# Scaled B and C variants of a state-space layer by TensorE rotation matrices, parameters by row loads

## Chip, cores, metric

The kernel runs on one core of one Trainium2 chip. The metric is device time in microseconds (us); lower is better. Executions of one kernel on one chip agree within two per cent here (the kernel before took 228.98 to 233.16 us in its widest group of runs), and each experiment below is compared with executions of the kernel before on the same chip. Engines are called by their names: TensorE (PE in the profile; PEld is its weight load), VectorE (DVE), ScalarE (ACT), GpSimd (POOL), SyncE (SP). ACTq and SPq are those engines' DMA issues.

## The reference

Two independent layers share the input length of 2048; their outputs stand side by side. Part A is a complex diagonal state-space layer, part B a sliding, dilated attention.

```python
# part A: 448 states, 448 features
dt = jnp.exp(log_dt)
Lam_bar = jnp.exp(dt * Lam)
B_bar = ((Lam_bar - 1.0) / Lam)[:, None] * Bmat
Bu = jnp.einsum("bld,pd->blp", x + 0j, B_bar)
for t in range(L):                      # h = Lam_bar * h + Bu[t], kept for every t
    ...
y = 2.0 * jnp.einsum("blp,dp->bld", hseq, Cmat).real + x * Dskip[None, None, :]
# part B: 16 heads of 28; each position sees 8 positions, 2 apart
logits = jnp.einsum("bhsd,bhswd->bhsw", q, kg) * scale
attn = _softmax(jnp.where(mask, logits, -1e9), axis=-1)
o = jnp.einsum("bhsw,bhswd->bhsd", attn, vg)   # then @ wo
```

The kernel takes part A in blocks. It needs four scaled variants of B (B times the powers 0, -1, -2, -3 of `Lam_bar`, with the factor of the third line) and three of C (times the powers 1, 2, 3). A state's real and imaginary parts are in partitions p and p + 64 of one of seven blocks `m`, so multiplying by a complex number mixes two partitions: it is a 2x2 rotation (with a scaling) for each state.

In what follows projection g makes q, k and v for group g of positions, units g are the four head groups of that group, and `wo` is the output projection. Part A runs in the order B variants, first layer, scan (the matrices `Mm` are its constants), `hfull`, `y`. An eviction is a copy out of PSUM, where the matmuls of these kernels leave their results.

## The kernel before

```python
# attention unit: one of 4 head groups of one of 5 groups of positions (cut)
def unit(self, gi, hg):
    ...                                   # scores by TensorE into s_ps
    for u in range(2):
        nc.scalar.activation(pt[...], sp[u][...], ACT.Exp, scale=scale)
        G.affine_select(out=pv, in_=pv, ...)      # band mask, one side
        G.affine_select(out=pv, in_=pv, ...)      # band mask, other side
    ...                                   # o_ps by TensorE
    V.transpose(tO, po); V.reciprocal(r, ...)
    V.tensor_tensor(on, tO, r, op=ALU.mult)       # both inputs in SBUF
    V.transpose(oT[:, hg, 0:tot], on)

# B variants: Re and Im swapped copy bY, then a multiply-add on VectorE, then a DMA transpose
def loads_b(self):
    ...
    for sl, v in ((slice(0, PL), bre_v), (slice(PL, P), bim_v)):
        nc.scalar.dma_start(self.bX[sl, :, 0:384], v[:, :, 0:384])
        nc.scalar.dma_start(self.bX[sl, :, 448:512], v[:, :, 384:448])
    nc.sync.dma_start(self.bY[0:PL], self.bX[PL:P])
    nc.sync.dma_start(self.bY[PL:P], self.bX[0:PL])

def b_variant(self, s):
    for m in range(NM):                                   # NM = 7
        # st = bX * sa   (ScalarE for even m, VectorE for odd m)
        eng.scalar_tensor_tensor(st[:, m, :], self.bY[:, m, :], self.sb[:, s, m:m + 1], st[:, m, :],
                                 op0=ALU.mult, op1=ALU.add)
    nc.sync.dma_start_transpose(self.Bv[s][:], st[:].rearrange("p m c -> p (m c)"))

# parameters: a column of two-byte elements for each partition
def loads_params(self):
    for src, name in ((self.A_Lre, "lre"), (self.A_Lim, "lim"), (self.A_logdt, "ldt")):
        v = src.rearrange("(m p) -> p m", p=PL)
        nc.sync.dma_start(raw[0:PL], v)
        nc.sync.dma_start(raw[PL:P], v)
    ...                                                   # dsk_raw in the same way

# ten matrices of powers for the scan: 128x896 each, two SBUF inputs, on GpSimd
def mats(self, eng):
    for i in range(NMAT):
        eng.tensor_tensor(self.M[:, i], self.Dm[...broadcast...], self.Sc[:, i]...broadcast..., op=ALU.mult)

# order of the program
b.loads(); a.loads_params(); b.load_x(0, 1); a.loads_b(); b.load_x(1, 0); b.load_x(1, 1)
b.prep(); a.setup(); b.proj(0); a.b_variant(0); a.loads_c()
for hg in range(4): b.unit(0, hg)
b.proj(1); a.b_variant(1); a.loads_x(); a.b_variant(2); b.loads2(); a.b_variant(3); a.mats(G)
for hg in range(4): b.unit(1, hg)
...     # projection 2, units 2 with the first layer l1, projection 3, scan l2, units 3,
...     # c_variants, hfull, y with units 4, output projections wo
```

The softmax here doesn't subtract the row's maximum and nothing guards it: scores larger than these inputs give would overflow.

Of the kernel before, what the change touches and what calls it, by code (L numbers as in the profile page):

```python
# [34 lines left out]
NMAT = len(MATS)  # L35

# [9 lines left out]
class PartB:  # L46
# [8 lines left out]
    def loads(self):  # L55
        nc, pool, G = self.nc, self.pool, self.nc.gpsimd
        self.xb = [pool.tile([P, KT, XC], bf16, name=f"xb{p}", tag=f"xb{p}") for p in range(2)]
        self.load_x(0, 0)
        self.wqk = pool.tile([P, KT, 2 * D], bf16, name="wqk_nat", tag="r3")
        self.wv = pool.tile([P, KT, D], bf16, name="wv")  # L60
        G.memset(self.wqk[0:64, 3, :], 0.0)
        G.memset(self.wv[0:64, 3, :], 0.0)
        w = self.B_wqkv
        nc.scalar.dma_start(self.wqk[:, 0:3, :], w[0:384, 0:2 * D].rearrange("(k p) c -> p k c", p=P))
        nc.scalar.dma_start(self.wqk[64:128, 3, :], w[384:448, 0:2 * D])
        nc.scalar.dma_start(self.wv[:, 0:3, :], w[0:384, 2 * D:].rearrange("(k p) c -> p k c", p=P))
        nc.scalar.dma_start(self.wv[64:128, 3, :], w[384:448, 2 * D:])
# [17 lines left out]
    def prep(self):  # L85
        nc, pool, V, G = self.nc, self.pool, self.nc.vector, self.nc.gpsimd
        for p in range(2):
            G.memset(self.xb[p][:, :, 0:XP], 0.0)
            G.memset(self.xb[p][:, :, XP + 1024:], 0.0)
        self.wp = pool.tile([P, 2, KT, H, 32], bf16, name="wqk_p", tag="wqk_p")  # L90
        G.memset(self.wp[:, :, :, :, DH:], 0.0)
# [4 lines left out]
    def proj(self, gi):  # L96
        nc, pool = self.nc, self.pool
# [17 lines left out]
        for w, segs, dst in ((0, qs, qT), (1, ks, kT)):  # L115
            for hg in range(4):
# [9 lines left out]
                n += 1  # L126
        nc.gpsimd.memset(va[:, :, :, DH:], 1.0)
        for i, (p, i0, _) in enumerate(blocks):
# [5 lines left out]
            if i % 2 == 0:  # L134
                nc.scalar.copy(va[:, i, :, 0:DH], ps[:])
            else:
                nc.vector.tensor_copy(va[:, i, :, 0:DH], ps[:])
# [58 lines left out]
class PartA:  # L196
# [8 lines left out]
    def loads_params(self):  # L205
        nc, pool = self.nc, self.pool
        self.raw = []
        for src, name in ((self.A_Lre, "lre"), (self.A_Lim, "lim"), (self.A_logdt, "ldt")):
            raw = pool.tile([P, NM], bf16, name=name + "_raw")
            v = src.rearrange("(m p) -> p m", p=PL)  # L210
            with nc.allow_non_contiguous_dma(reason="tiny param vector"):
                nc.sync.dma_start(raw[0:PL], v)
                nc.sync.dma_start(raw[PL:P], v)
            self.raw.append(raw)
        self.dsk_raw = pool.tile([P, KT], bf16, name="dsk_raw")
        with nc.allow_non_contiguous_dma(reason="tiny param vector"):
            nc.sync.dma_start(self.dsk_raw[:, 0:3], self.A_Dskip[0:384].rearrange("(k p) -> p k", p=P))
            nc.sync.dma_start(self.dsk_raw[:, 3:4], self.A_Dskip[320:448].rearrange("(k p) -> p k", p=P))

    def loads_b(self):  # L220
        nc, pool = self.nc, self.pool
        self.bX = pool.tile([P, NM, 512], bf16, name="bX", tag="r0")
        self.bY = pool.tile([P, NM, 512], bf16, name="bY", tag="r1")
        nc.gpsimd.memset(self.bX[:, :, 384:448], 0.0)
        bre_v = self.A_Bre.rearrange("(m p) d -> p m d", p=PL)
        bim_v = self.A_Bim.rearrange("(m p) d -> p m d", p=PL)
        for sl, v in ((slice(0, PL), bre_v), (slice(PL, P), bim_v)):
            nc.scalar.dma_start(self.bX[sl, :, 0:384], v[:, :, 0:384])
            nc.scalar.dma_start(self.bX[sl, :, 448:512], v[:, :, 384:448])
        nc.sync.dma_start(self.bY[0:PL], self.bX[PL:P])  # L230
        nc.sync.dma_start(self.bY[PL:P], self.bX[0:PL])
# [9 lines left out]
    def loads_c(self):  # L241
        nc, pool = self.nc, self.pool
        cn = pool.tile([112, 4, NM, 2, PL], bf16, name="cn", tag="c7")
        with nc.allow_non_contiguous_dma(reason="interleaving re and im columns"):
            for ri, src in enumerate((self.A_Cre, self.A_Cim)):
                for a in range(4):
                    nc.gpsimd.dma_start(cn[:, a, :, ri, :],
                                        src[112 * a:112 * (a + 1)].rearrange("p (m q) -> p m q", q=PL))
        self.cP = pool.tile([P, NM, D], bf16, name="cP")
        self.cQ = pool.tile([P, NM, D], bf16, name="cQ")  # L250
        for a in range(4):
            nc.sync.dma_start_transpose(self.cP[:, :, 112 * a:112 * (a + 1)],
                                        cn[:, a].rearrange("p m r q -> p (m r q)"))
        nc.sync.dma_start(self.cQ[0:PL], self.cP[PL:P])
        nc.sync.dma_start(self.cQ[PL:P], self.cP[0:PL])

    def setup(self):
# [6 lines left out]
        lre, lim, ldt = sm("lre"), sm("lim"), sm("ldt")  # L264
        for t_, r_ in zip((lre, lim, ldt), self.raw):
            V.tensor_copy(t_[:], r_[:])
        dsk = sm("dsk", (P, KT))
        V.tensor_copy(dsk[:], self.dsk_raw[:])
        dt_bf = pool.tile([P, NM], bf16, name="dt_bf")
        nc.scalar.activation(dt_bf[:], ldt[:], ACT.Exp)  # L270
# [6 lines left out]
        V.tensor_tensor(arg[:], dt[:], lre[:], op=ALU.mult)  # L277
        th = sm("th")
        V.tensor_tensor(th[:], dt[:], lim[:], op=ALU.mult)
# [33 lines left out]

        lm1, den, t0, t1, rden = sm("lm1"), sm("den"), sm("t0"), sm("t1"), sm("rden")
        V.tensor_scalar(lm1[:], la_re, -1.0, None, op0=ALU.add)
        V.tensor_tensor(den[:], lre[:], lre[:], op=ALU.mult)
        V.tensor_tensor(t0[:], lim[:], lim[:], op=ALU.mult)
        V.tensor_tensor(den[:], den[:], t0[:], op=ALU.add)
        V.reciprocal(rden[:], den[:])
        sa, sb, tb = sm("sa", (P, 4, NM)), sm("sb", (P, 4, NM)), sm("tb", (P, 3, NM))  # L320
        g_re, g_im = sa[:, 0, :], sb[:, 0, :]
        V.tensor_tensor(g_re, lm1[:], lre[:], op=ALU.mult)
        V.tensor_tensor(t1[:], la_im, lim[:], op=ALU.mult)
        V.tensor_tensor(g_re, g_re, t1[:], op=ALU.add)
        V.tensor_tensor(g_re, g_re, rden[:], op=ALU.mult)
        V.tensor_tensor(g_im, la_im, lre[:], op=ALU.mult)
        V.tensor_tensor(t1[:], lm1[:], lim[:], op=ALU.mult)
# [3 lines left out]
        b3 = [P, 3, NM]  # L331
# [7 lines left out]
        V.tensor_scalar(sb[0:PL], sb[0:PL], -1.0, None, op0=ALU.mult)  # L339
        self.sa, self.sb = sa, sb  # L340
        self.ca, self.cb = sm("ca", b3), sm("cb", b3)
        V.tensor_scalar(self.ca[0:PL], pw_re[0:PL, 0:3, :], 2.0, None, op0=ALU.mult)
        V.tensor_scalar(self.ca[PL:P], pw_re[PL:P, 0:3, :], -2.0, None, op0=ALU.mult)
        V.tensor_scalar(self.cb[:], pw_im[:, 0:3, :], -2.0, None, op0=ALU.mult)
# [6 lines left out]
        Sc = pool.tile([P, NMAT, NM, 2], bf16, name="Sc")  # L351
        V.tensor_copy(Sc[0:PL, :, :, 0], pw_re[0:PL, 3:13])
        V.tensor_scalar(Sc[PL:P, :, :, 0], pw_im[PL:P, 3:13], -1.0, None, op0=ALU.mult)
        V.tensor_copy(Sc[0:PL, :, :, 1], pw_im[0:PL, 3:13])
        V.tensor_copy(Sc[PL:P, :, :, 1], pw_re[PL:P, 3:13])  # L355
        self.Sc = Sc
        self.Dg = pool.tile([P, KT, P], bf16, name="Dg")
        for k in range(KT):
            V.tensor_scalar(self.Dg[:, k, :], ident[:], dsk[:, k:k + 1], None, op0=ALU.mult)
        V.memset(self.Dg[0:PL, 3, :], 0.0)  # L360

    def mats(self, eng):
        self.M = self.pool.tile([P, NMAT, NM, 2, PL], bf16, name="Mm")
        for i in range(NMAT):
            eng.tensor_tensor(self.M[:, i], self.Dm[:].unsqueeze(1).unsqueeze(1).to_broadcast([P, NM, 2, PL]),  # L365
                              self.Sc[:, i].unsqueeze(3).to_broadcast([P, NM, 2, PL]), op=ALU.mult)
# [4 lines left out]
    def b_variant(self, s):  # L371
        nc, pool, eng = self.nc, self.pool, self.nc.vector
        if s == 0:
            self.Bv = [None] * 4
        st = pool.tile([P, NM, 512], bf16, name="st", tag=("r2" if s % 2 == 0 else "r3"))
        for m in range(NM):
            if m % 2 == 0:
                nc.scalar.activation(st[:, m, :], self.bX[:, m, :], ACT.Copy, scale=self.sa[:, s, m:m + 1])  # L378
            else:
                eng.tensor_scalar(st[:, m, :], self.bX[:, m, :], self.sa[:, s, m:m + 1], None, op0=ALU.mult)  # L380
            eng.scalar_tensor_tensor(st[:, m, :], self.bY[:, m, :], self.sb[:, s, m:m + 1], st[:, m, :],  # L381
                                     op0=ALU.mult, op1=ALU.add)
        self.Bv[s] = pool.tile([P, NM * KT, P], bf16, name=f"Bv{s}", tag=f"Bv{s}")
        nc.sync.dma_start_transpose(self.Bv[s][:], st[:].rearrange("p m c -> p (m c)"))

    def c_variants(self):
        nc, pool = self.nc, self.pool
        self.Dv = [self.cP]
        for s in range(1, 4):
            d = pool.tile([P, NM, D], bf16, name=f"Dv{s}", tag=f"Bv{s}")  # L390
            for m in range(NM):
                nc.scalar.activation(d[:, m, :], self.cP[:, m, :], ACT.Copy, scale=self.ca[:, s - 1, m:m + 1])  # L392
                nc.vector.scalar_tensor_tensor(d[:, m, :], self.cQ[:, m, :], self.cb[:, s - 1, m:m + 1], d[:, m, :],  # L393
                                         op0=ALU.mult, op1=ALU.add)
            self.Dv.append(d)
        for m in range(NM):
# [194 lines left out]
```

## Time and profile before

The time is 233.42 us (median of 2, 233.21 to 233.62); the profiled execution has a span of 229.9 us. The first line of the page gives each engine's busy time, its share of the span and its instructions.

```profile
PE 162.8 (71%) x1298; PEld 83.2 (36%) x1298; DVE 152.8 (66%) x271; ACT 102.9 (45%) x179; POOL 129.1 (56%) x149
```

No engine is busy all the time, so shares of the span do not say what a change is worth. The next table cuts the span into stretches: for each, its length, the busy time of each engine with its count of instructions, TensorE's mean granted clock (PEclk; 1.00 is full speed), the share of time that the DMA engines were busy and GB/s.

```profile
core 0: us, PE busy (x) PEld busy (x) DVE busy (x) ACT busy (x) POOL busy (x), PEclk, DMA share, GB/s
0.00:33.00 33.00, 12.98 (x64) 5.59 (x65) 15.80 (x75) 8.82 (x17) 17.54 (x48) 0.84 1.11 182
33.00:91.00 58.00, 34.16 (x282) 14.06 (x281) 58.00 (x58) 29.20 (x46) 54.66 (x38) 0.78 0.64 116
91.00:147.00 56.00, 52.67 (x402) 25.28 (x403) 35.39 (x63) 34.00 (x59) 21.37 (x24) 0.95 0.13 29
147.00:192.00 45.00, 30.88 (x302) 19.43 (x300) 33.55 (x54) 20.77 (x39) 27.74 (x24) 0.62 0.06 15
192.00:229.00 37.00, 32.16 (x253) 18.84 (x251) 10.08 (x24) 10.06 (x21) 7.80 (x16) 1.00 0.21 66
```

From 33 to 91 us VectorE is busy all the time, and TensorE a little over half. From 91 to 147 and from 192 on TensorE is the limit. The groups of instructions show what fills VectorE (busy time, mean ns of one; then the idle time of the engine just before these instructions and what ended it).

```profile
L381 DVE SCALAR_TENSOR_TENSOR st<-bY,sb,st 128x512 bf16<-128x512 bf16 x28 | 38.4, 1408 | 0.0
L120 PE MATMUL qk_ps<-xb_66,wqk_p 128*128 128x480 bf16 (+5 forms) x96 | 23.5, 392 | 19.1 <-ACT qT L125 9.6
L365 POOL TENSOR_TENSOR Mm<-Dm,Sc 128x896 bf16<-128x896 bf16 x10 | 19.5, 1980 | 12.9 <-DVE Sc L355 12.9
L180 DVE TENSOR_TENSOR on<-tO,r 128x480 bf16<-128x480 f32 (+2 forms) x20 | 18.3, 917 | 0.3
```

The 28 multiply-adds `st` of the B variants take 38.4 us, and TensorE waits once for 9.6 us for ScalarE's first eviction `qT`.

### The profile page before, as it was taken

The page shows a single profiled execution, that of the slowest core. Times are in us where ns is not written, and L with a number is a line of the kernel's source. Part 1 is how long each engine was busy: PE and PEld are TensorE (multiplying, and loading weights), DVE is VectorE, ACT ScalarE, POOL GpSimd, SP SyncE. Part 2 cuts the span into 40 slices and gives each one's busy share as a digit, 9 for nine tenths or more (in the row PEclk, how much of TensorE's full clock was granted, in tenths as well). Part 3 has the DMA queues.
Part 4 walks back from the last instruction along what each step waited for, and adds up shares of the span by engine and source line. Part 5 has one row for each costly group of instructions (what it writes and reads, how often), then busy time and mean ns, then how long its engine had stood idle before and what let it go on. Part 6 is the DMA issues. An engine that isn't in the chain of part 4 may idle for free.

```text
span 229.9 us, 3506 instructions
## 1 busy us (share of the span) xinstructions
PE 162.8 (71%) x1298; PEld 83.2 (36%) x1298; DVE 152.8 (66%) x271; ACT 102.9 (45%) x179; POOL 129.1 (56%) x149
## 2 busy tenths in 40 slices
PE   0512947577593480999999999859943498998894
PEld 0200423232241130443344345635511294555562
DVE  0324999999999999965365277866999912152240
ACT  0004488537177050463552699992411353403313
POOL 8980029999999995653615520199996003213300
PEclk9975899659689587699999999965575569999999
DMA  6999999998480070820000000200020000211223
GB/s 192 152 155 196 197 195 139 200 235 152 84 161 0 0 148 14 160 75 3 0 0 3 0 1 0 73 0 4 20 55 0 0 3 7 76 60 45 76 65 99
DMA packets 46313, 17.50 MB, mean 76 GB/s; under 512 B 39784, under 2 KB 45672, under 8 KB 46296
## 3 DMA queue, kind: packets, MB, share of 16 engines
q1 hardware_dynamic: 42904, 14.07, 31.9%
q10 hardware_dynamic: 2816, 2.01, 4.3%
q0 software_dynamic: 576, 1.21, 3.3%
q8 instruction: 10, 0.16, 0.3%
q14 instruction: 7, 0.06, 0.1%
HBM read 3.22 MB, written 3.67 MB: 30 GB/s over the span
## 4 chain that ended last, share of the span: by engine, by line
DVE 35%; PE 26%; POOL 11%; ACT 9%; issue 2%; DMA 1%; ACTq 0%; DVEq 0%
DVE st L381 15%; PE y_ps L468 7%; POOL pt L162 6%; PE l_ps L409 6%; DVE on L180 5%; POOL pt L164 3%; DVE st L380 3%; PE o_ps L170 3%; DVE Dv_1839 L393 3%; ACT pt L160 3%; PE wo_ps L189 3%; PE qk_ps L120 2%; DVE tO L176 2%; DVE oT L181 2%; POOL cP L397 2%
## 5 line engine op out<-in xcount | busy, mean ns | idle before, releaser
L162 POOL TENSOR_SCALAR_AFFINE_SELECT pt<-pt 128x960 bf16<-128x960 bf16 (+2 forms) x40 | 41.6, 1062 | 59.2 <-ACT pt L160 59.2
L160 ACT ACTIVATE pt<-s_ps 128x960 bf16<-128x960 f32 (+2 forms) x40 | 32.1, 859 | 40.0 <-PE o_ps L170 21.4
L164 POOL TENSOR_SCALAR_AFFINE_SELECT pt<-pt 128x960 bf16<-128x960 bf16 (+2 forms) x40 | 41.4, 1058 | 0.0
L381 DVE SCALAR_TENSOR_TENSOR st<-bY,sb,st 128x512 bf16<-128x512 bf16 x28 | 38.4, 1408 | 0.0
L120 PE MATMUL qk_ps<-xb_66,wqk_p 128*128 128x480 bf16 (+5 forms) x96 | 23.5, 392 | 19.1 <-ACT qT L125 9.6
L170 PE MATMUL o_ps<-pt,va 128*32 128x120 bf16 (+2 forms) x288 | 12.7, 251 | 29.1 <-DVE tO L176 16.5
L120 PEld LDWEIGHTS <-wqk_p 128*128 128x128 bf16 x192 | 18.3, 117 | 37.7 <-issue 29.2
L365 POOL TENSOR_TENSOR Mm<-Dm,Sc 128x896 bf16<-128x896 bf16 x10 | 19.5, 1980 | 12.9 <-DVE Sc L355 12.9
L170 PEld LDWEIGHTS <-va 128*32 128x32 bf16 x288 | 8.0, 108 | 42.7 <-issue 22.1
L120 PE MATMUL qk_ps<-xb_67,wqk_p 128*128 128x480 bf16 (+5 forms) x96 | 21.6, 363 | 1.9 <-ACT qT L125 1.9
L176 DVE STREAM_TRANSPOSE tO<-o_ps 128x480 f32<-128x480 f32 (+2 forms) x20 | 12.0, 600 | 12.8 <-PE o_ps L170 12.7
L397 POOL TENSOR_SCALAR cP<-cP,sgn_212 128x448 bf16<-128x448 bf16 x7 | 10.6, 1532 | 14.3 <-ACT Dv_1839 L392 14.3
L189 PE MATMUL wo_ps<-wo_p,oT 128*120 128x448 bf16 (+2 forms) x72 | 18.5, 404 | 0.0
L180 DVE TENSOR_TENSOR on<-tO,r 128x480 bf16<-128x480 f32 (+2 forms) x20 | 18.3, 917 | 0.3
L192 ACT CAST yb<-wo_ps 120x448 bf16<-120x448 f32 (+2 forms) x18 | 9.8, 546 | 16.0 <-PE wo_ps L189 15.2
L153 PE MATMUL s_ps<-qT,kT 28*128 28x120 bf16 (+2 forms) x288 | 14.6, 234 | 0.6 <-ACT pt L160 0.5
L478 DVE CAST ya<-y_ps 128x448 bf16<-128x448 f32 x8 | 5.0, 623 | 13.7 <-PE y_ps L472 13.7
L378 ACT ACTIVATE st<-bX,sa 128x512 bf16<-128x512 bf16 x16 | 10.9, 725 | 3.5 <-DMA bY<-bX 2.4
L189 PEld LDWEIGHTS <-oT 128*120 128x120 bf16 (+2 forms) x72 | 10.2, 149 | 5.1 <-issue 0.7
L153 PEld LDWEIGHTS <-kT 28*128 28x128 bf16 x288 | 7.5, 100 | 12.1 <-issue 10.9
L181 DVE STREAM_TRANSPOSE oT<-on 128x480 bf16<-128x480 bf16 (+2 forms) x20 | 11.7, 585 | 0.2
L125 ACT CAST kT<-qk_ps 128x488 bf16<-128x488 f32 (+2 forms) x20 | 10.3, 527 | 3.1 <-PE qk_ps L120 2.9
(166 smaller groups left out, 286.0 us busy)
## 6 DMA issues: line engine op xcount, KB each, us to landing
out_dram<-ya SPq DMA_DIRECT2D x16, 112.0 KB, 1.7
bY<-bX SPq DMA_DIRECT2D x2, 448.0 KB, 5.4
out_dram<-yb SPq DMA_DIRECT2D x8, 105.0 KB, 1.8
cQ<-cP SPq DMA_DIRECT2D x2, 392.0 KB, 4.8
out_dram<-yb SPq DMA_DIRECT2D x8, 98.0 KB, 1.8
wqk_nat<-in_B_wqkv_dram ACTq DMA_DIRECT2D x1, 672.0 KB, 4.2
cn<-in_A_C_re_dram POOLq DMA_DIRECT2D x4, 98.0 KB, 6.1
cn<-in_A_C_im_dram POOLq DMA_DIRECT2D x4, 98.0 KB, 7.1
```

What stands on the lines that cost most here:

```text
L120: nc.tensor.matmul(ps[:, off:off + cnt], lhsT=self.wp[:, w, k, 4 * hg:4 * hg + 4].rearrange("p h d -> p (h d)"), rhs=self.xb[p][:, k, XP + ...
L153: nc.tensor.matmul(sp[h // 2][:, h % 2, nq * i:nq * (i + 1)], lhsT=kT[32 * h:32 * h + DH, hg, koff[i]:koff[i] + P], rhs=qT[32 * h:32 * h + ...
L160: nc.scalar.activation(pt[:, :, 0:tot], sp[u][:, :, 0:tot], ACT.Exp, scale=scale)
L162: G.affine_select(out=pv, in_=pv, compare_op=ALU.is_ge, fill=0.0, base=-1, pattern=[[0, 2], [0, nb], [-1, nq]], channel_multiplier=1)
L164: G.affine_select(out=pv, in_=pv, compare_op=ALU.is_ge, fill=0.0, base=HALO, pattern=[[0, 2], [0, nb], [1, nq]], channel_multiplier=-1)
L170: nc.tensor.matmul(po[32 * h:32 * h + 32, nq * i:nq * (i + 1)], lhsT=va[:, i, 4 * hg + h, :], rhs=pts[h // 2][:, h % 2, nq * i:nq * (i + 1 ...
L176: V.transpose(tO[:, 0:nj].rearrange("p j d -> p (j d)"), po[:, 0:tot])
L180: V.tensor_tensor(on[:, 0:nj], tO[:, 0:nj], r[:, 0:nj].unsqueeze(2).to_broadcast([P, nj, 32]), op=ALU.mult)
L181: V.transpose(oT[:, hg, 0:tot], on[:, 0:nj].rearrange("p j d -> p (j d)"))
L189: nc.tensor.matmul(ps[0:nq, :], lhsT=oT[:, hg, nq * i:nq * (i + 1)], rhs=self.wo_p[:, hg, :], start=(hg == 0), stop=(hg == 3))
L365: eng.tensor_tensor(self.M[:, i], self.Dm[:].unsqueeze(1).unsqueeze(1).to_broadcast([P, NM, 2, PL]), self.Sc[:, i].unsqueeze(3).to_broadca ...
L381: eng.scalar_tensor_tensor(st[:, m, :], self.bY[:, m, :], self.sb[:, s, m:m + 1], st[:, m, :], op0=ALU.mult, op1=ALU.add)
```

## The change

The intent: a rotation by 2x2 blocks is a matrix, so TensorE can make the variants. `MB` and `MC` hold the matrices; B variants come out of PSUM already transposed, so the swapped copies and the DMA transposes go too. VectorE and ScalarE only evict. Parameters come as 28 rows of 128 bytes, which TensorE turns. The order of the program changes along with it: all B variants after the first four attention units, the first layer no longer between units, two output projections earlier.

Cut from the diff below are smaller edits: all evictions of v go to ScalarE, a dummy exp loads ScalarE's table at the start, and some memsets change engine.

```diff
     def loads_params(self):
-        for src, name in ((self.A_Lre, "lre"), (self.A_Lim, "lim"), (self.A_logdt, "ldt")):
-            ...                                  # 8 loads of two-byte elements, on SyncE
+        self.pr = pool.tile([NPR, P], bf16, name="pr")
+        for i, src in enumerate((self.A_Lre, self.A_Lim, self.A_logdt, self.A_Dskip)):
+            nc.scalar.dma_start(self.pr[NM * i:NM * (i + 1), 0:PL], src.rearrange("(m p) -> m p", p=PL))

     def loads_b(self):
-        ...                                      # 4 bX loads on ScalarE, 2 swapped copies bY on SyncE
+        nc.gpsimd.dma_start(self.bX[0:PL], self.A_Bre.rearrange("(m p) d -> p m d", p=PL))
+        nc.gpsimd.dma_start(self.bX[PL:P], self.A_Bim.rearrange("(m p) d -> p m d", p=PL))

-    def b_variant(self, s):
-        ...                                      # st = bX*sa + bY*sb, DMA transpose
+    def b_variant(self, m):
+        for k in range(KT):
+            nc.tensor.matmul(ps[:]..., lhsT=self.bX[:, m, c0:c0 + P], rhs=self.MB[:, m]..., start=True, stop=True)
+            if k % 2 == 0:
+                nc.scalar.copy(dst, ps[lo:P])
+            else:
+                nc.vector.tensor_copy(dst, ps[lo:P])

     def c_variants(self):                        # likewise: 21 matmuls with MC, evictions shared
+        # and cP is scaled by one VectorE instruction instead of seven on GpSimd

 # order
-    b.prep(); a.setup(); b.proj(0); a.b_variant(0); a.loads_c()
+    b.prep(); b.load_x(0, 1); a.loads_b(); a.setup()   # after three steps of projection 0
+    b.load_x(1, 0); b.load_x(1, 1); a.b_mats(V); a.loads_x()
     for hg in range(4): b.unit(0, hg)
-    b.proj(1); a.b_variant(1); a.loads_x(); a.b_variant(2); b.loads2(); a.b_variant(3); a.mats(G)
+    a.loads_c()
+    for m in range(NM): a.b_variant(m)
+    b.loads2(); a.setup_dg(); b.proj(1); a.mats(G); a.c_transpose()
     for hg in range(4): b.unit(1, hg)
     ...
```

## The prediction

> **What bounds it now.** No engine bounds the whole span of 229.9 us (first part of the page: TensorE 71%, VectorE 66%, GpSimd 56%). The stage table gives four regimes. 33-91 us: VectorE is busy 100%; the chain of waits there is almost all `st` (28 scalar-tensor-tensor, mean 1408 ns by shape, 38.4 us, plus 9.0 us of scaling). First-layer matmuls wait for its last variant until about 100 us. 91-147 us: TensorE, 95% busy at clock 0.96. 147-176 us: scan, `Dv` and softmax tail, VectorE and GpSimd, clock 0.62. 192-227 us: TensorE again (`y`, then 24 `wo` matmuls).
>
> The Trainium skill, "SBUF — State Buffer", "Who interferes with whom", says that a VectorE operation with two SBUF inputs contends with a GpSimd operation that reads SBUF. The trace agrees: a band select takes 1.46 us beside `st` but 1.0 us at 110 us; the same `Dv` update 0.68 us alone, about 1.2 us beside GpSimd.
>
> **Removed.** `st` on VectorE 47.4 us, on ScalarE 10.9 us; `Dv` on VectorE 16 us, ScalarE 14 us; cP scaling on GpSimd 10.6 us; four Bv transposes, bY and cQ copies; 3200 two-byte packets of parameter loads, whose last landing (19.8 us) stops ScalarE, and through PSUM TensorE, for 9.6 us.
>
> **Added.** 28 matmuls of 512 columns and 21 of 448, 0.19-0.21 us each when warm: 10 us of TensorE. 49 PSUM evictions at 0.53-0.69 us: about 15 us each for ScalarE and VectorE. Seven rotation builds on VectorE, 0.6-1.5 us each, and one cP scaling (about 2 us, estimated from 0.35 us per 512 columns).
>
> **Critical path, by stages (estimates from those durations).** First unit's softmax starts at about 26 us instead of 34. But VectorE's queue holds the cP scaling before the first attention transpose, and cP is the 17th to 20th transpose on its queue; at 1.3-1.5 us per issue it lands near 40 us. So the second unit's output waits until about 43 us and GpSimd idles some us. VectorE then owes MB, four unit tails and 14 evictions, about 22 us: Bv complete near 65 us, projection 1 done near 76 us. (In the kernel before, projection 1 was done near 62 us: part of the gain is given back.) Then TensorE-bound: units 1, wo 0, first layer, projection 2, units 2, wo 1, projection 3: 58 us of full-clock work, at the 89% efficiency that 96-147 us shows, 65 us: scan starts near 141 us (147 before). Scan to last `hl` update is VectorE-bound: 37 us of its work, so `y` starts near 183 us (192). `y` loses two interleaved units and the tail 16 `wo` matmuls: about 31 us from `y` to end instead of 38. Sum: span about 212 us, time about 215.
>
> **Right or wrong shows in.** No 9.6 us TensorE gap at 12-21 us; a VectorE wait on the cP transpose of 8-14 us before 43 us; selects near 1.0-1.2 us; VectorE busy 125-135 us, ScalarE slightly up, GpSimd about 110; first-layer matmuls starting 78-85 us; scan near 141; clock still 0.5-0.7 in scan and `hl` stages (the skill, "TensorE: Matmul & The Clock Gate", Part 1: idleness re-gates the clock; here 0.54-0.61 at 150-190 us).
>
> **Wrong if** cP lands much earlier or later than 40 us; TensorE stays half-clocked through the Bv stage and projection 1 (slower by 5-8 us); evictions alternating over three PSUM buffers stall more than summed; or the scan and `Dv` evictions overlap better than a VectorE-serial sum (faster by 8 us).
>
> Prediction: 215 us, 203 to 226 eight times in ten; faster by over 2%: 0.93, within 2%: 0.06, slower: 0.01.

## More of the kernel before

A piece of ScalarE's stream at the head, in order of time (start, duration), is:

```profile
14.49 0.60 ACTq L228 DMA_DIRECT2D bX<-in_A_B_im_dram  x1
19.13 0.61 ACTq L229 DMA_DIRECT2D bX<-in_A_B_im_dram  x1
19.77 1.28 ACT L270 ACT_TABLE_LOAD   x1 [19.77 <-DMA dsk_raw<-in_A_Dskip_dram]
21.06 0.21 ACT L270 ACTIVATE dt_bf<-ldt 128x7 bf16<-128x7 f32 x1
21.18 0.54 ACT L125 CAST qT<-qk_ps 128x480 bf16<-128x480 f32 x1
```

Two readings are possible. The bracket puts the wait down to the last parameter's landing; but the lines above it show ScalarE's own DMA issues, the last of them at 19.13, and the first eviction stands behind them in the same stream. The prediction took the first reading. The experiments e6 to e8 below bear on it.

## The result, and the profile after

The changed kernel takes 248.2 us (median of 2, 248.06 and 248.35): slower by 6.3%. The ratio is 1.0634, 95% interval 1.0586 to 1.0682. Here and below a ratio is the mean time of one kernel's fast runs over the mean of the other's fast runs of the same rounds, so it is not quite the ratio of the medians that are quoted. Executions over 1.5% slower than the fastest of the same kernel are left out of the means. The busy times after:

```profile
PE 172.6 (70%) x1348; PEld 85.7 (35%) x1348; DVE 137.1 (56%) x243; ACT 102.1 (41%) x177; POOL 115.5 (47%) x140
```

TensorE got 10 us more, VectorE 16 us less and GpSimd 14 us less, near what was predicted (VectorE's sum has a wait of 15 us in it, shown below). The sums look right and the time is wrong, so the loss is in when things run. The stretches after, in the same columns as before:

```profile
core 0: us, PE busy (x) PEld busy (x) DVE busy (x) ACT busy (x) POOL busy (x), PEclk, DMA share, GB/s
0.00:36.00 36.00, 15.11 (x65) 6.08 (x66) 13.65 (x65) 8.27 (x17) 12.87 (x40) 1.00 1.07 182
36.00:62.00 26.00, 7.80 (x101) 3.75 (x101) 25.83 (x33) 8.40 (x12) 24.99 (x21) 0.59 0.34 57
62.00:79.00 17.00, 1.11 (x17) 0.44 (x17) 17.00 (x5) 0.54 (x1) 17.00 (x11) 0.50 0.05 13
79.00:103.00 24.00, 19.74 (x86) 7.43 (x85) 12.60 (x20) 12.45 (x23) 0.98 (x4) 0.73 0.00 1
103.00:128.00 25.00, 23.24 (x201) 10.54 (x188) 13.19 (x22) 12.94 (x20) 16.54 (x17) 0.93 0.06 18
128.00:172.00 44.00, 41.55 (x295) 19.63 (x294) 14.59 (x22) 26.23 (x44) 17.49 (x17) 0.96 0.03 10
172.00:214.00 42.00, 36.16 (x389) 21.57 (x388) 31.52 (x62) 25.92 (x51) 21.66 (x24) 0.92 0.06 17
214.00:246.00 32.00, 27.91 (x215) 16.24 (x213) 8.78 (x18) 7.35 (x16) 3.96 (x8) 0.99 0.21 70
```

Between 62 and 79 us VectorE is "busy" all of 17 us with five instructions, and TensorE works for 1.1 us. One VectorE instruction is most of it:

```profile
62.03 15.26 DVE L187 TENSOR_TENSOR on<-tO,r 128x480 bf16<-128x480 f32 x1
```

Beside it, on GpSimd, the ten `Mm` builds run one after the other:

```profile
61.98 16.85 POOL L353 TENSOR_TENSOR Mm<-Dm,ScM 128x896 bf16<-128x896 bf16 x10
```

`on` takes 0.62 us when it is let in at once (as in experiment e9, at 61.77). Here it waited while nine builds of 1.67 to 1.70 us passed, and was done 0.55 us after the tenth had started. Behind it in VectorE's queue stand the evictions of `Bv`, so TensorE all but stops (it waited 16.9 us for VectorE's `Bv` evictions), as the groups show:

```profile
L395 PE MATMUL bv_ps<-MB,bX 128*128 128x512 bf16 x28 | 13.3, 576 | 27.8 <-DVE Bv L402 16.9
L129 PE MATMUL qk_ps<-xb_66,wqk_p 128*128 128x480 bf16 (+5 forms) x96 | 20.8, 369 | 13.7 <-DMA xb_66<-in_B_x_dram 13.6
L353 POOL TENSOR_TENSOR Mm<-Dm,ScM 128x896 bf16<-128x896 bf16 x10 | 16.8, 1721 | 0.0
L187 DVE TENSOR_TENSOR on<-tO,r 128x480 bf16<-128x480 f32 (+2 forms) x20 | 30.0, 1502 | 0.3
```

The group `on` went from 18.3 to 30.0 us with the same 20 instructions. The trap in reading this page: a group's busy time includes the waiting for a port, and the engine appears to be fully used.

The second loss is at the head. ScalarE's stream after:

```profile
1.90 0.82 ACTq L216 DMA_DIRECT2D pr<-in_A_Lambda_re_dram  x1
...
4.88 0.28 ACTq L216 DMA_DIRECT2D pr<-in_A_Lambda_im_dram  x1
14.95 0.27 ACTq L216 DMA_DIRECT2D pr<-in_A_log_dt_dram  x1
22.27 0.27 ACTq L216 DMA_DIRECT2D pr<-in_A_Dskip_dram  x1
...
23.70 1.48 ACT L134 CAST qT<-qk_ps 128x480 bf16<-128x480 f32 x3 [20.93 <-DMA pr<-in_A_Dskip_dram]
```

Each issue itself takes 0.27 us, but the third comes 10 us after the second and the fourth 7 us after that. SyncE's stream has these at the same time:

```profile
7.78 6.86 SPq L85 DMA_TRANSPOSE xb_66<-in_B_x_dram  x1
14.68 5.40 SPq L84 DMA_TRANSPOSE xb_67<-in_B_x_dram  x1
```

The eight parameter loads of the kernel before were on SyncE; their four replacements are in ScalarE's stream and come while SyncE's transposes are being issued. That the transposes hold them is read from these times alone: in e1, where the head is the same, the third issue came at 14.86 us and the transpose beside it was being issued until 14.93; no run took the transposes away. The first eviction, which was at 21.18, comes at 23.70 us, and the first exp at 36.0 (34.0 before).

Milestones in us from the start of the span, all from the traces (e1, e3, e5, e10 are experiments below):

| | before | predicted | after | e1 | e3 | e5 | e10 |
|---|---|---|---|---|---|---|---|
| first `qT` eviction | 21.2 | | 23.7 | 24.5 | 10.6 | 10.5 | 9.6 |
| first exp | 34.0 | 26 | 36.0 | 36.4 | 21.8 | 21.2 | 21.1 |
| last B eviction | | 65 | 94.2 | 79.3 | 77.1 | 64.4 | 66.5 |
| first exp of units 1 | 63.2 | 76 | 103.3 | 88.5 | 87.5 | 73.4 | 48.5 |
| scan starts | 145.3 | 141 | 172.4 | 157.9 | 156.6 | 144.1 | 136.7 |
| `y` starts | 191.2 | 183 | 213.6 | 200.5 | 197.7 | 186.2 | 176.3 |
| span | 229.9 | 212 | 246.3 | 233.3 | 230.4 | 218.9 | 208.9 |

The column "predicted" gives projection 1 done for the first exp of units 1, which is the same point within about a microsecond or two.

### The profile page after: what moved, and what is told of

It is laid out like the page before. It is cut to its first block, busy times and chain, and to the rows that moved or that the text cites. A ratio compares the mean times of both kernels' runs of the same rounds, so it can differ in the third digit from the quotient of the medians.

```text
span 246.3 us, 3528 instructions
## 1 busy us (share of the span) xinstructions
PE 172.6 (70%) x1348; PEld 85.7 (35%) x1348; DVE 137.1 (56%) x243; ACT 102.1 (41%) x177; POOL 115.5 (47%) x140
## 3 DMA queue, kind: packets, MB, share of 16 engines
q1 hardware_dynamic: 24792, 8.67, 18.3%
q0 software_dynamic: 800, 2.01, 4.5%
## 4 chain that ended last, share of the span: by engine, by line
PE 40%; DVE 21%; POOL 15%; SPq 12%; DMA 5%; ACT 4%; issue 1%; ACTq 0%; DVEq 0%
PE l_ps L430 10%; DVE on L187 9%; POOL pt L171 8%; PE y_ps L489 8%; POOL pt L169 7%; PE qk_ps L129 7%; PE v_ps L141 4%; SPq L85 4%; DMA xb_67<-in_B_x_dram 4%; DVE MB L353 3%; PE bv_ps L395 3%; SPq L229 3%; ACT pt L167 2%; SPq L230 2%; SPq L84 2%; DVE tO L183 2%
## 5 line engine op out<-in xcount | busy, mean ns | idle before, releaser
L395 PE MATMUL bv_ps<-MB,bX 128*128 128x512 bf16 x28 | 13.3, 576 | 27.8 <-DVE Bv L402 16.9
L129 PE MATMUL qk_ps<-xb_66,wqk_p 128*128 128x480 bf16 (+5 forms) x96 | 20.8, 369 | 13.7 <-DMA xb_66<-in_B_x_dram 13.6
L187 DVE TENSOR_TENSOR on<-tO,r 128x480 bf16<-128x480 f32 (+2 forms) x20 | 30.0, 1502 | 0.3
L430 PE MATMUL l_ps<-xa,Bv 128*128 128x512 bf16 x112 | 28.1, 395 | 0.2 <-DVE hl_941 L436 0.2
L129 PEld LDWEIGHTS <-wqk_p 128*128 128x128 bf16 x192 | 16.9, 106 | 30.4 <-issue 13.5
L400 ACT CAST Bv<-bv_ps 128x512 bf16<-128x512 f32 x14 | 8.2, 586 | 32.6 <-PE bv_ps L395 32.5
L134 ACT CAST qT<-qk_ps 128x480 bf16<-128x480 f32 (+2 forms) x20 | 9.8, 502 | 27.5 <-DMA pr<-in_A_Dskip_dram 20.9
L129 PE MATMUL qk_ps<-xb_67,wqk_p 128*128 128x480 bf16 (+5 forms) x96 | 19.1, 332 | 0.0
L177 PEld LDWEIGHTS <-va 128*32 128x32 bf16 x288 | 7.7, 103 | 26.5 <-issue 17.1
L353 POOL TENSOR_TENSOR Mm<-Dm,ScM 128x896 bf16<-128x896 bf16 x10 | 16.8, 1721 | 0.0
L430 PEld LDWEIGHTS <-Bv 128*128 128x128 bf16 x112 | 10.9, 101 | 14.2 <-issue 3.5
L395 PEld LDWEIGHTS <-bX 128*128 128x128 bf16 x28 | 3.3, 120 | 35.4 <-issue 35.4
```

The source lines that it names most:

```text
L129: nc.tensor.matmul(ps[:, off:off + cnt], lhsT=self.wp[:, w, k, 4 * hg:4 * hg + 4].rearrange("p h d -> p (h d)"), rhs=self.xb[p][:, k, XP + ...
L134: nc.scalar.copy(dst[:, hg, 0:tot], ps[:, 0:tot])
L177: nc.tensor.matmul(po[32 * h:32 * h + 32, nq * i:nq * (i + 1)], lhsT=va[:, i, 4 * hg + h, :], rhs=pts[h // 2][:, h % 2, nq * i:nq * (i + 1 ...
L187: V.tensor_tensor(on[:, 0:nj], tO[:, 0:nj], r[:, 0:nj].unsqueeze(2).to_broadcast([P, nj, 32]), op=ALU.mult)
L353: eng.tensor_tensor(out, self.Dm[:].unsqueeze(1).unsqueeze(1).to_broadcast([P, NM, 2, PL]), Sc[:, i].unsqueeze(3).to_broadcast([P, NM, 2, ...
L395: nc.tensor.matmul(ps[:].rearrange("p s c -> p (s c)"), lhsT=self.bX[:, m, c0:c0 + P], rhs=self.MB[:, m].rearrange("p s h q -> p (s h q)") ...
```

## The experiments

Eleven runs were made, in three groups, all with correct results. The kernel before took 231.34 us in the first group (e1 to e4), 231.86 in the second (e0, e5 to e7) and 230.56 in the third (e8 to e10).

The theory after the result had two parts. S: VectorE's `on` is starved by the uninterrupted run of two-input builds on GpSimd. H: the loads' issues in ScalarE's stream hold the head. The rivals were that GpSimd's and VectorE's work costs this much wherever it stands, and that the DMA traffic itself sets the head.

### e0: the changed kernel again

No edit; four executions beside e5.

> The changed kernel again, unedited, so that it stands on the chip of the runs beside it. It was 6.3% slower than the kernel before on another chip. If the 15.3 us wait of one `on` comes with every execution, the ratio is 1.05 to 1.08 and the same `on` or its neighbour is again over 10 us long. If the wait depends on the moment at which VectorE arrives and that moment differs from chip to chip, the ratio may fall to 1.02 or the long wait may sit on another instruction.

Measured: 247.53 (the profiled one), 247.39, 248.18 and 235.94 us. The kernel before stayed within 4.2 us on the same chip. So this is read as two courses of the same program, 12 us apart. No ratio is given. The profiled execution has the long wait again (`on` at 60.88, 15.29 us). That the 235.94 us execution lacked it is inferred from the size alone, for it has no trace.

### e1: builds taken off GpSimd

```diff
-    a.mats(G)
+    a.mats(V)      # on VectorE, made to wait for the last Bv eviction by a factor 1.0 computed from Bv
```

> Edit: the ten scan matrices Mm are built on VectorE after the last Bv eviction instead of on GpSimd after the first four units; VectorE's order is otherwise that of the changed kernel. Theory S (starved port: the normalisation `on` that ran 15.3 us from 62.0 us waited because ten GpSimd builds ran back to back on the shared SBUF port): longest `on` 2 us or less, Bv complete near 78 us instead of 93, and the ten builds fit in VectorE's idle time of 93-103 us at 1.07 us each; span falls by 12 to 15 us, time 233 to 236. Rival W (that `on` waits for something else, such as a semaphore, and GpSimd is innocent): `on` is still about 15 us long, time 248 or more.

Measured: 234.0 us, ratio 1.0116 (1.0051 to 1.0181). The longest `on` takes 1.49 us. The groups:

```profile
L187 DVE TENSOR_TENSOR on<-tO,r 128x480 bf16<-128x480 f32 (+2 forms) x20 | 14.9, 744 | 0.3
L353 DVE TENSOR_TENSOR Mm<-Dm,ScM 128x896 bf16<-128x896 bf16 x10 | 10.1, 1084 | 0.0
```

`on` is halved, from 30.0 us. The ten builds cost VectorE 10.1 us, less than the 16.8 us that they take on GpSimd, and the last B eviction comes at 79.3 instead of 94.2 us: 15 us earlier, from an edit that adds 10 us of work to VectorE. S holds in so far as the builds on GpSimd make the wait; that the work as such costs the time is ruled out. (Whether the row has to be uninterrupted is the question of e2 and e9.)

### e2: short gaps between the builds

```diff
             self.build(eng, self.M[:, i], self.ScM, i)
+            eng.memset(gap[:], 0.0)      # one column
```

> Edit: a one-column memset of an unused tile after each of the ten Mm builds on GpSimd, which stay where they are. If the port is kept only because one reading GpSimd instruction follows the other with no gap, a write-only instruction in between lets VectorE in: longest `on` about 2 us as in the kernel before, Mm 1.7 to 2.1 us each, time 234 to 238. If VectorE is shut out for as long as GpSimd's queue is not empty, `on` stays at 15 to 17 us, time 248 to 250.

Measured: 247.11 (profiled) and 242.34 us; no ratio is given, and the expected numbers were missed. In the profiled run an `on` that arrived 0.05 us into the first build got in after that build (2.17 us), a second one took 1.42, but the third, at 71.40, took 10.41 us, past the end of the last build. So memsets of 0.09 us do not keep VectorE from a long wait.

### e9: long gaps between the builds

```diff
             self.build(eng, self.M[:, i], self.ScM, i)
+            eng.memset(gap[:], 0.0)      # 128x960 bf16
```

> Changed kernel with a write-only memset of 128x960 bf16 (about 0.9 us, estimated from 1.61 us for 128x1792) after each Mm build on GpSimd, where e2 had 0.09 us. Theory G (VectorE gets in whenever GpSimd stops reading SBUF for long enough): no VectorE operation between the first and the last build takes over 2.7 us, Bv complete at 78 to 84 us, all times at 233 to 239 us, none near 247. Rival (a waiting operation is let in only by the order in which it came, whatever the gaps): one VectorE operation again lasts over 8 us until the last build ends, and times stand at 245 to 252 us or fall into two groups as in e0.

Measured: 249.5 us, ratio 1.082 (1.0779 to 1.0862); theory G fell and its rival's numbers came. VectorE in this kernel:

```profile
61.77 0.62 DVE L187 TENSOR_TENSOR on<-tO,r 128x480 bf16<-128x480 f32 x1
...
67.24 0.69 DVE L404 CAST Bv<-bv_ps 128x512 bf16<-128x512 f32 x1
67.85 18.93 DVE L187 TENSOR_TENSOR on<-tO,r 128x480 bf16<-128x480 f32 x1
```

And GpSimd in the same time:

```profile
67.22 1.68 POOL L353 TENSOR_TENSOR Mm<-Dm,ScM 128x896 bf16<-128x896 bf16 x1
68.85 0.89 POOL L374 MEMSET gap<- 128x960 bf16 x1
...
84.59 1.68 POOL L353 TENSOR_TENSOR Mm<-Dm,ScM 128x896 bf16<-128x896 bf16 x1
```

The waiting instruction outlasted seven gaps, each longer than the 0.62 us that it needs, and ended about when the last build did. In the same stretch the first `on` ran in 0.62 us, though it arrived 0.05 us into a build. So the waiting instruction is not simply let in whenever GpSimd writes only. It can lose to a whole row of instructions. What decides between getting in at once, after one build and after all of them, these runs do not settle.

Which instructions are hit is clear. `Bv` evictions, which read PSUM, took 0.69 us beside builds as elsewhere, e.g. the one at 67.24 us above. The instructions that waited were `on`, with two SBUF inputs, and in e3 the scaling of `cP`, 128x3136 from SBUF to SBUF. This agrees with the Trainium skill, "SBUF — State Buffer", "Who interferes with whom", which says that VectorE instructions with at most one SBUF input, outside the fast modes with two ports, do not contend with GpSimd, and that those with two SBUF inputs contend with a GpSimd instruction that reads SBUF. The scaling has a single tensor as input, so it fits only if it ran in such a mode. No view states that; its pace suggests it (3136 elements of each partition in 1.03 us in e5, where `on` takes 0.62 us for 480).

### e3: parameter and wv loads issued by GpSimd

```diff
-            nc.scalar.dma_start(self.pr[...], ...)      # four loads
+            nc.gpsimd.dma_start(self.pr[...], ...)
-        nc.scalar.dma_start(self.wv[...], ...)          # two loads
+        nc.gpsimd.dma_start(self.wv[...], ...)
```

> Edit: the four parameter row loads and the two wv loads are issued by GpSimd instead of ScalarE. Theory H (ScalarE's own DMA issues are held up to 22 us behind the transposes of the other queue, so the engine cannot evict the first projection): first qT eviction near 15 us instead of 23.7, TensorE gap at 18-26 us gone, first exp near 27 us instead of 36, time 4 to 9 us lower than 248.2, unless the Mm builds starve a later `on` all the same. Rival D (the data itself lands late because the DMA engines are full): first exp still at 33 to 36 us, time within 2 us of 248.

Measured: 232.21 us, ratio 1.0039 (0.9974 to 1.0105). ScalarE's first eviction comes at 10.56 us and the first exp at 21.8, 14 us earlier than after and earlier than the 15 and 27 us expected: H holds. (In the six runs that leave the head alone, after, e0, e1, e2, e4 and e9, the first exp comes at 34.6 to 39.3 us.) The same bytes moved; what changed is the stream that issues them, and with it their DMA queue, from a hardware queue to the software queue in the page's list. In the program as built the edit also changed an order: the last load of C stands behind the selects, and the scaling of `cP`, at 44.49 us ahead of the `Bv` evictions in the kernel after, came at 59.87 us, ahead of the last five of VectorE's. The starvation did not go, it fell on another instruction: the scaling of `cP` (TENSOR_SCALAR, 128x3136), which takes 1.82 us in the changed kernel and 1.03 in e5, started at 59.87 us and took 13.06. It ran until 72.93, 1.99 us after the last build ended at 70.94.

### e4: other loads after the builds

```diff
-    b.loads2()
     a.setup_dg()
     b.proj(1)
     a.mats(G)
+    b.loads2()       # GpSimd's issues of wo_p behind the builds instead of ahead of them
```

> Edit: the four wo_p loads are issued by GpSimd after the ten Mm builds instead of before them; VectorE's order is the same. The builds then start about 2.4 us earlier, at about 59.6 us, so `on` reaches the port in the middle of a build, as in the kernel before, not 50 ns after one began. If starvation depends on the moment of arrival or on the descriptor work ahead of the builds, the longest `on` falls to about 2 us and time to 234 to 238. If back-to-back builds always starve it, `on` is about 12 to 15 us and time 245 to 248.

Measured: 237.4 us, ratio 1.0262 (1.0165 to 1.0359). The builds stay on GpSimd, in a row, from 62.85 to 80.94 us, at 1.81 us each; the longest `on` is 1.94 us. So the row does not always starve VectorE. The builds did not start 2.4 us earlier as expected, for in this execution the head, which the edit leaves alone, came 3.4 us later than after (first exp at 39.3 us). With e0 this suggests that a profile of such a kernel can look harmless in one execution and not in the next.

### e5: e1 and e3 together

> Edit: the changed kernel with both cures: the Mm builds on VectorE after the last Bv eviction, and the parameter and wv loads issued by GpSimd. If the head (first exp 36 us, 14 us late) and the starved port (13 to 15 us) are two separate costs that add up, first exp is near 22 us, Bv complete near 62 to 64 us and the span near 216 to 219 us: 5 to 6% under the kernel before. Rival: the stages after Bv are bound by TensorE and by the scan in a way that gives the gain back, and the time stays at 228 to 233 us.

Measured: 219.4 us (218.08 to 220.95, six executions), ratio 0.9491 (0.9428 to 0.9554). From the 247.5 us of e0's profiled course on the same chip, this is 28 us; the two edits alone gave about 13.5 (e1) and 15.3 (e3). They add up, and together they turn 6% slower into 5% faster. (The ratios of fast runs say the same: from 1.0634 in the result, e1 takes off 0.052, e3 0.060 and both 0.114.) The time lies within the range that the prediction gave, in part by luck: its stretches miss by -5 to +6 us and cancel in part (last column of the table below, against "predicted"), and `cP` is scaled behind the `Bv` evictions here as in e3.

### e6 and e7: the two readings of the head of the kernel before

e6 takes the kernel before and issues the four `bX` loads from GpSimd:

```diff
-            nc.scalar.dma_start(self.bX[sl, :, 0:384], v[:, :, 0:384])      # and the second of each pair
+            nc.gpsimd.dma_start(self.bX[sl, :, 0:384], v[:, :, 0:384])
```

> Edit to the kernel before: only the four bX loads are issued by GpSimd instead of ScalarE; the two-byte parameter loads stay. My prediction put the 9.6 us TensorE gap at 12 to 21 us down to the parameter loads. If ScalarE is instead held by its own bX issues (the last at 19.1 us), the first qT eviction comes near 13 us instead of 21.2, first exp near 27 to 30 us, time 1 to 5 us lower (VectorE's st stage still follows the setup chain). If the parameters hold it, the first eviction stays near 20 us and the time within 1%.

Measured: 242.23 us, ratio 1.0476 (1.0398 to 1.0554); missed. ScalarE's second `wv` issue now came at 14.80, the parameters landed later, and ScalarE waited 8.0 us for `ldt`; its first eviction was at 26.5.

e7 takes the kernel before and replaces the two-byte parameter loads by row loads, still on SyncE:

```diff
-                nc.sync.dma_start(raw[0:PL], v)          # and the other seven
+            nc.sync.dma_start(self.pr[NM * i:NM * (i + 1), 0:PL], src.rearrange("(m p) -> m p", p=PL))
```

> Edit to the kernel before: the parameter loads alone are done as in the change (four row loads of 128-byte rows, transposed by TensorE), on the SyncE queue where they were; nothing else. If the two-byte packets are what costs (they hold the DMA engines and the last lands at 19.4 us), the parameters land by 10 us, the gap shrinks and time falls 3 to 8 us. If ScalarE's own bX issues hold it, first eviction stays at 18 to 21 us and time changes less than 2%, in spite of 3200 fewer packets.

Measured: 235.11 us, ratio 1.0172 (1.0112 to 1.0233). The parameters were there and turned by TensorE at 11.78, and still ScalarE's first eviction came only at 19.78. Its stream:

```profile
17.74 0.60 ACTq L220 DMA_DIRECT2D bX<-in_A_B_im_dram  x1
18.37 1.28 ACT L262 ACT_TABLE_LOAD   x1 [18.37 <-DMA bX<-in_A_B_re_dram]
```

The table load starts 0.03 us after the last `bX` issue ends, as it did in the kernel before (19.13 + 0.61, then 19.77). So there the issue held the stream, and the parameters, which were ready for ScalarE about 16.5 us after the start, held nothing that the issue didn't hold longer. Removing the slow parameter loads alone gains 1.4 us at the first eviction and nothing in the time.

### e8: all these loads of the kernel before issued by GpSimd

The edits of e6 and e7 together, with parameter rows and `wv` issued by GpSimd too.

> Kernel before with both heads' holds taken away together: parameter row loads, wv loads and bX loads all issued by GpSimd. Theory D (two holds stand side by side in ScalarE's stream in the kernel before, the parameters by way of dt_bf and ScalarE's own bX issues, and each alone is enough to hold its first eviction until about 20 us): with both gone the first qT eviction is at 11 to 15 us (21.2 in before, 26.5 and 19.8 in the two single edits) and the first exp at 22 to 27; VectorE's st chain then starts at 26 to 31 (33.9) and the time is 225 to 231. Rival (the DMA engines' load or the arrival of x, not the order of issues, sets the head): first eviction stays at 18 or later and the time at 233 or more.

Measured: 243.38 us, ratio 1.0548 (1.0497 to 1.0598); missed, and the experiment does not separate what it was meant to. In the program as built, sixteen DMA transposes of x instead of five now stand ahead of the copies `bY` in SyncE's stream (issued at 42.4 us, 24.9 before), so the multiply-adds of the B variants began at 49.3 instead of 33.9 us; and VectorE makes `Dg` (14.6 to 18.3 us) ahead of the chain that ScalarE's `ex` waits for, which in turn stands ahead of the first eviction (19.3 us). It shows only that fewer DMA issues in ScalarE's stream do not help if waits for VectorE stand in their place.

### e10: e5 with projection 1 among the first units

```diff
     for hg in range(4):
         b.unit(0, hg)
+        if hg == 1:
+            b.proj(1)
 ...
-    b.proj(1)          # after the B variants
```

> e5 with projection 1 issued between the second and third attention unit of group 0 instead of after the Bv matmuls. In e5 TensorE is idle for about 11 us between 30 and 44 us behind VectorE's setup chain and does projection 1 at 65 to 73 us. If TensorE is the limit from Bv on: first exp of units 1 at 65 to 69 us (73.4), everything after 4 to 7 us earlier, time 212 to 216 against 219.4. If VectorE's Bv evictions and Mm builds set the pace there (VectorE was busy 9.6 of 10 us at 60 to 70): the units gain less than 2 us and the time stays at 217 to 220.

Measured: 211.4 us (210.63 to 212.14, six executions), ratio 0.9166 (0.9135 to 0.9196): 8.3% faster than the kernel before, the fastest of all. In e5 VectorE's setup leaves TensorE idle; two stretches of e5 and e10 show it:

```profile
core 0: us, PE busy (x) PEld busy (x) DVE busy (x) ACT busy (x) POOL busy (x), PEclk, DMA share, GB/s
21.00:64.00 43.00, 19.86 (x147) 7.13 (x143) 40.31 (x72) 15.48 (x23) 27.82 (x27) 0.56 0.53 93
```

```profile
core 0: us, PE busy (x) PEld busy (x) DVE busy (x) ACT busy (x) POOL busy (x), PEclk, DMA share, GB/s
21.00:66.00 45.00, 32.75 (x266) 12.29 (x266) 40.76 (x70) 25.79 (x41) 31.10 (x33) 0.72 0.50 87
```

TensorE does 13 us more in nearly the same time, at a granted clock of 0.72 instead of 0.56. More than the projection moved: units 1 began at 48.5 us, between the B variants, and the last B eviction was 2 us later than in e5. The milestone that was expected to come 4 to 8 us earlier came 25 earlier; the time that was expected (212 to 216) was slightly beaten. One long wait is still there: an `on` at 51.59 us took 5.23 us, while five band selects of 0.98 to 1.01 us each, which have a single input, ran in a row on GpSimd. So it is not a matter of the builds alone, nor of two inputs on GpSimd's side, and a next version should look at the selects too.

## Why the prediction was wrong

The prediction's sum, stretch by stretch (differences of its milestones and of the measured ones):

| stretch | predicted | after | off by | e5 |
|---|---|---|---|---|
| start to first exp | 26 | 36.0 | +10.0 | 21.2 |
| first exp to last B eviction | 39 | 58.2 | +19.2 | 43.2 |
| to first exp of units 1 | 11 | 9.1 | -1.9 | 9.0 |
| to scan | 65 | 69.1 | +4.1 | 70.7 |
| scan to `y` | 42 | 41.2 | -0.8 | 42.1 |
| `y` to end | 29 | 32.7 | +3.7 | 32.7 |
| span | 212 | 246.3 | +34.3 | 218.9 |

**The step that failed most: "VectorE then owes MB, four unit tails and 14 evictions, about 22 us: Bv complete near 65 us".** It added durations and left out the waiting for GpSimd. About 15 of the 19 us are the one wait of `on`; e1 removes it and gets the last B eviction 15 us earlier. The prediction had quoted the right page, and even measured the effect: selects at 1.46 instead of 1.0 us, `Dv` at 1.2 instead of 0.68. It took contention for a factor of 1.5 to 2 on each instruction. In the kernel before that was all there was, as `Mm` builds and `st` took turns (builds of 1.98 us mean). The longest VectorE instruction of its whole trace takes 2.17 us, so it shows no wait that outlasts one GpSimd instruction, although it has a bare row of builds too, nine of them with no select in between:

```profile
56.50 17.83 POOL L365 TENSOR_TENSOR Mm<-Dm,Sc 128x896 bf16<-128x896 bf16 x9
```

```profile
62.78 2.13 DVE L180 TENSOR_TENSOR on<-tO,r 128x480 bf16<-128x480 f32 x1
```

This `on` and the next (66.60 us, 2.01 us) waited for one build each. So the trace at hand gave no sign of a wait for a whole row, and the row by itself does not make it: of the runs with a row on GpSimd, after, e0, e2, e3 and e9 have the long wait, and before, e4, e6, e7 and e8 do not.

**The other 4 us of that stretch** are put down to the setup on VectorE beside the selects. A 128x7 product takes 0.15 us at 36.54 us and 1.00 us at 37.69, as soon as selects run; the four `MB` builds took 7.4 us, 1.90 us on average, outside the 0.6 to 1.5 us that the prediction allowed. This is argued and not tested: in e5 the four took 1.07 us each, and the stretch is still 4 us over. TensorE's half clock in it (below) is a rival.

**The second step that failed: "3200 two-byte packets of parameter loads, whose last landing (19.8 us) stops ScalarE".** The page's bracket names that landing; the stream shows ScalarE's own `bX` issue ending at 19.74, just before. The last landing is `dsk_raw`, which ScalarE's next instruction does not even read. e7 shows it: without those packets the first eviction still waits for the last issue. The change removed the `bX` issues from ScalarE's stream but put the parameter loads there, and these were held in the same way, until 22.27 us. So the head came out 10 us later than predicted, and e3 shows that moving the issues, with the bytes unchanged, cures it. It cures it better than predicted: 21.8 instead of 26 us.

**Predicted and not seen: "a VectorE wait on the cP transpose of 8-14 us before 43 us".** VectorE came to the scaling of `cP` at 44.49 without idle time ahead of it, its setup being late by the head and the selects; the transposes had been issued from 37.1 to 41.1. (In e0, e1, e2 and e4 it waited 0.9 to 1.3 us.) A wait that was to be the limit vanished because its rival was slower.

**Mis-sized: TensorE's stretch, "at the 89% efficiency that 96-147 us shows, 65 us".** It measured 69.1, and 70.7 in e5. In e5 the part from 74 to 100 us has a granted clock of 0.80 against 0.96 in the 44 us after it. If that factor alone counts, 26 us at 0.80 hold 4.3 us less work than at 0.96 (26 x 0.16 / 0.96, an estimate from these two clocks). In the kernel after, the clock of this stretch is 0.93 to 0.96, so its own 4.1 us stay open. Also the end from `y` on: 32.7, where the text said 31 and its milestones left 29.

**Right, in part by luck:** the total work. GpSimd at about 110 us (115.5 measured), VectorE at 125 to 135 (137.1). But 14.6 us of the 137.1 are the wait of the one `on`: without it 122.5 us are left, below the range (e4, without a long wait, has 123.4), so VectorE's near agreement is luck; ScalarE "slightly up" was 102.1 against 102.9, so level. The late stages: scan to `y` at 42 us was right to a microsecond (45.9 before), though not for the reason given: VectorE, held to be the limit with 37 us of work, was busy for 31.5 of the 42 us from 172 to 214, and TensorE for 36.2. `y` to end fell by 6 us against the kernel before (32.7 against 38.7), less than the 7 of the text. The clock of the scan stage was expected at 0.5 to 0.7 and measured 0.92, where TensorE was busier than before (36.2 of 42 us, against 30.9 of 45). The skill, "TensorE: Matmul & The Clock Gate", Part 1, which says that an idle TensorE gets the throttled clock, agrees in the other place: with TensorE nearly idle from 62 to 79 us the clock was 0.50. The prediction listed a half clock through the Bv stage and projection 1 as a risk of 5 to 8 us. It came in the Bv stage, but not by the starvation alone: the clock was 0.57 from 79.0 to 94.2 us after, and without the long wait still 0.54 in e1 (62.0 to 79.3) and 0.61 in e5 (48.0 to 64.4). From the last B eviction to the first exp of units 1, where projection 1 runs, it was 1.00 in all three.

**What stays open:** why one arrival gets in at once, another after one build and another after all. The moment of arrival within a build does not decide it: 0.18 us into one, `on` waited for that build alone in the kernel before (66.60 us) and for the rest of the row in e2 (71.40 us); and GpSimd's spans are rough in these profiles. Open too is whether the 235.94 us execution of e0 was one without the long wait.

## What to carry to other kernels

A row of GpSimd instructions that read SBUF is a risk beside a queue of VectorE that feeds TensorE: one VectorE instruction of two SBUF inputs may wait for the whole row (15.26 us here), with everything behind it, and gaps in the row did not help in e2 and e9; ten builds on VectorE cost 10 us there and saved 15. A quiet trace of the same row proves little, for the kernel before had one. A DMA issue in the stream of a computing engine is an instruction, and two of them came 10 us apart here; put the loads of the head in the stream of an engine that has nothing urgent, and look at the engine's own issues before believing the name in the bracket. When the sums of a profile look right and the time is wrong, look for the longest single instruction.

## What the Trainium skill lacked or had wrong

- "SBUF — State Buffer", "Who interferes with whom": says that whoever issues first holds the shared ports "for the whole instruction". It does not say that the loser can wait for many consecutive instructions of the other engine: 15.26 us over nine builds (after), 13.06 us (e3), 10.41 us (e2), 18.93 us (e9), 5.23 us over five band selects (e10), where the instruction alone takes 0.62 us, or 1.03 us for the scaling that waited in e3 (as in e5).
- The same section: a VectorE instruction with two SBUF inputs contends with GpSimd instructions that read SBUF, "not with one that only writes it". In e9 such an instruction, already waiting, was not let in during seven write-only memsets of 0.89 us each.
- The same section: "Issue order, not op shape, decides who blocks." Issue order alone does not foretell the length: an arrival 0.05 us into a build took 0.62 us (e9), 2.17 us (e2), 15.26 us (after).
- "DMA: Bandwidth & Descriptors", "Issuing engines are not separate DMA queues": says that issuing from several engines only saves the sequencer's time, usually small. Here the choice of the issuing engine moved the first exp by 14 us (e3), where issues of 0.27 us in ScalarE's stream came 10 and 7 us apart while transposes of 6.86 and 5.40 us were being issued on SyncE (after). That section tells of no such hold.
